# Gate products of feed-forward block i paired with the up products of block i-1, and a new constant for the pace of exponentials in the build-time model

## The chip, the cores and the metric

The kernel runs on one core of a Trainium2 chip, in one launch. The metric is device time in microseconds: 844.57 as the median of four runs (843.4 to 848.04). In the text PE is the matrix engine, DVE the vector engine, ACT the scalar engine, POOL the GpSimd engine, and SP the engine that issues most of the DMAs.

## What is computed

An input x of 2048 rows and 512 columns goes through multi-head attention (32 heads of width 16, no mask) and, beside it, through a feed-forward layer of width 1792 with a SiLU gate. A sigmoid of one dot product for each row mixes the two. All arrays are bfloat16.

```python
qkv = (x @ wqkv).reshape(B, S, 3, H, Dh).transpose(2, 0, 3, 1, 4)      # B=1, S=2048, H=32, Dh=16
p = softmax(einsum("bhqd,bhkd->bhqk", q, k) * Dh ** -0.5)
a = einsum("bhqk,bhkd->bhqd", p, v).transpose(0, 2, 1, 3).reshape(B, S, D) @ wo
b = (silu(x @ w_gate) * (x @ w_up)) @ w_down                            # 512 -> 1792 -> 512
g = sigmoid((x * gate_w).sum(-1, keepdims=True))
return g * a + (1 - g) * b
```

## The kernel before

**Attention.** Queries are cut into four blocks of 512 (`qb`) and heads into eight groups of four (`g`); a pair (qb, g) is a unit, and there are 32 units of 16 key tiles of 128 keys, so 512 tiles of four heads each. A tile goes one of two ways. On the ACT way (`emit_pair`, L698, twice for a tile) PE makes the scores of two heads into a 128x1024 tile `s_t`, of which there are two, and ACT takes the exponential of it into `e_t`. On the DVE way (`emit_d`, L731) PE makes the four scores of a tile one by one into a 128x512 bank `d_t`, and DVE makes the exponential by arithmetic on the bits: four times `y_t<-d_t`, then over 2048 columns `z_t`, a line `u_t`, its square, its product with `z_t`, a POOL DMA that adds it to `y_t`, and a last scaling. The scratch tile of the line bears the name `u_t`, `kaug` or `wd_t`, after where it lies. PE then multiplies either kind with the values into `o_ps` (`pv`, L838).

**Banks.** `d_t`, the feed-forward products and all small products share three PSUM banks (`ps_m`, handed out by `m_tile`, given back by `m_free`).

**Feed-forward.** For each of the four query blocks there are 14 blocks of 128 gate and up columns, 56 in all. `gu_chain` (L619) makes the products of one block with `two_banks` (L378): eight pieces, each a pair of matmuls that run beside each other on the two halves of the array's rows, one into the gate's bank `gu_a` and one into the up's bank `gu_b`. After the last piece ACT takes `th` = tanh(gate/2), DVE makes `gs` = (th + 1) * gate, and then `mt` = 0.5 * gs * up. Both banks are held until DVE has read them. After 14 blocks the products with w_down follow (`down_pieces`, L653, banks `dps_a` and `dps_b`, copied out into `bblk`). The chains run one after the other: each has the one before in its list `after`, and is ready only when that one's pieces are out and all that it owes to DVE has been put in order.

**The order of the work.** The order of the instructions on PE, DVE and ACT is worked out at build time and written as a fixed order (`ordered`, L145). A small model (`Plan`, L276) counts on a clock for each engine: `spend` for PE, `spend_v` for DVE, and on ACT `plan.act`, by `ACT_US` = 0.935 for each exponential of 128x1024 and 0.48 for a tanh. The loop at L1300 puts a pair of scores when the model says that a tile `s_t` comes free, and fills the room before that (`room`, L1310) with DVE-way scores, products with the values, and pieces of the chains. DVE's work waits in the lists `owed` (by a due time), `d_wait`, `vops` and `added`, and `fill_dve` (L802) puts it as long as DVE's clock is behind PE's. `v_unit` (L1267) says whether DVE may take a further tile from the end of a unit: its clock and its work in hand plus `LEAD` = 16 us must lie before the end of that unit's exponentials, counted by `TILE_US` = 1.87 for each tile left.

**Weights.** `load` issues on SP's queue the two 128 KB loads of a block, two blocks ahead, into three buffers each for `wg` and `wu`.

**The end.** `tail` (L939) puts in order what is left of the chains before the last product with the values, and half of the last output products.

Of the kernel before, what the change touches and what calls it, by code (L numbers as in the profile page):

```python
# [9 lines left out]
ALU = mybir.AluOpType  # L10
AX = mybir.AxisListType
BF16 = mybir.dt.bfloat16
# [66 lines left out]
def kernel(  # L79
# [12 lines left out]
    nc = tc.nc  # L92
    P = 128
    x = A_x.flatten_outer_dims()
    S, D = x.shape
    F = B_w_gate.shape[1]
# [4 lines left out]
    DC = D // P  # L101
    FC = F // P
    KT = S // P
    QBW = 512
    QB = S // QBW
# [26 lines left out]
    work = ctx.enter_context(tc.tile_pool(name="work", bufs=2))  # L132
    etp = ctx.enter_context(tc.tile_pool(name="etp", bufs=EB))
    vex = ctx.enter_context(tc.tile_pool(name="vex", bufs=1))
    ffnw = ctx.enter_context(tc.tile_pool(name="ffnw", bufs=3))
# [20 lines left out]
    def mm(*args, **kw):  # L156
        return ordered(nc.tensor.matmul(*args, **kw))  # L157
# [10 lines left out]
    vec = Ordered()  # L168


    xT = big.tile([P, DC, S], BF16, name="xT")
# [37 lines left out]
    mt = big.tile([P, FC, QBW], BF16, name="mt")  # L209
# [39 lines left out]
    for h in range(8):  # L249
        c = 2 * (h % 4) + h // 4  # L250
# [38 lines left out]
    def spend(mode, mms, ready=0.0):  # L289

        plan.seq += 1
        work_at.append((plan.pe, mms))
        plan.pe = max(plan.pe + (0.1 if mode != plan.mode else 0.0), ready) + (0.226 if mode == "F" else 0.216) * mms
        plan.mode = mode

    def later(cost, f, ready=None, key=None):

        c = plan.chain
        if c is not None:
            c.owed += 1  # L300
        ready = plan.pe + 0.25 if ready is None else ready
        owed.insert(sum(o[0] <= ready for o in owed), (ready, cost, f, c, key))
# [8 lines left out]
    def pay(i=0):  # L311
        ready, cost, f, c, key = owed.pop(i)
        spend_v(cost, ready, key)
        keep, plan.chain = plan.chain, None
        f()
        plan.chain = keep
        if c is not None:
            c.owed -= 1
            if c.done():
                c.done_at = plan.slot  # L320
# [14 lines left out]
    def m_tile(name):  # L335
        while m_ready() is None:
            stuck()
        i = min((i for i in range(3) if banks[i] is not None), key=lambda i: banks[i])
        plan.pe = max(plan.pe, banks[i])
        banks[i] = None  # L340
        held[i] = ps_m[i].tile([P, QBW], F32, tag=f"m{i}", name=name)
        return held[i]

    def m_free(ps, t):
        i = [h is ps for h in held].index(True)
        banks[i], held[i] = t + 0.2, None
# [11 lines left out]
    def force(c):  # L358
        for a in c.after:
            force(a)  # L360
        while not c.out():
            while c.cond is not None and not c.cond():
                if owed:
                    pay()
                else:
                    for f in at.pop(min(at)):
                        f()
            emit_piece(c)
        while c.owed:
            pay()  # L370
# [7 lines left out]
    def two_banks(n, name, a, b, end, stop=True):  # L378

        st = {}  # L380

        def pc(k):
            v, i = divmod(k, n)

            def f():
                if k == 0:
                    while m_ready(2) is None:
                        stuck()
                    st["a"], st["b"] = m_tile(name + "_a"), m_tile(name + "_b")
                if k == n:  # L390
                    sync(ordered(nc.tensor.nop()), st["half"])
                    spend("R", 0.1 if st["seq"] < plan.seq else 1.5)
                for ps, (w, r), h in ((st["a"], a(i), v), (st["b"], b(i), 1 - v)):
                    rows = slice(64 * h, 64 * h + 64)
                    st["half"] = mm(ps[:, :], lhsT=w[rows, :], rhs=r[rows, :], start=(k == i == 0),
                                    stop=(stop and k == 2 * n - 1), tile_position=(64 * h, 0), skip_group_check=True)
                spend("R", 1)
                st["seq"] = plan.seq
                if k == 2 * n - 1:
                    end(st["a"], st["b"])  # L400
            return f
        return [(1, pc(k), 2 if k == 0 else 0, "R", st if k == n else None) for k in range(2 * n)]
# [213 lines left out]
        later(0.5, end, plan.act + 0.2)  # L616


    def gu_chain(qb, fc):  # L619
        st = {}  # L620

        def load():
            st["wg"] = ffnw.tile([P, DC, P], BF16, tag="wg", name="wg")
            nc.sync.dma_start(out=st["wg"][:], in_=B_w_gate[:, fc * P:(fc + 1) * P].rearrange("(dc p) f -> p dc f", p=P))
            st["wu"] = ffnw.tile([P, DC, P], BF16, tag="wu", name="wu")
            nc.sync.dma_start(out=st["wu"][:], in_=B_w_up[:, fc * P:(fc + 1) * P].rearrange("(dc p) f -> p dc f", p=P))

        def rows(which):
            return lambda dc: (st["w" + which][:, dc, :], xT[:, dc, qb * QBW:(qb + 1) * QBW])

        def done_gu(gp, up):
            th = work.tile([P, QBW], BF16, tag="th", name="th")
            flush_act(plan.pe + 0.4)
            act(out=th[:], in_=gp[:, :], func=ACT.Tanh, scale=0.5)
            plan.act = max(plan.act, plan.pe + 0.25) + 0.48

            def gate():
                st["gs"] = work.tile([P, QBW], BF16, tag="gs", name="gs")
                vec.scalar_tensor_tensor(out=st["gs"][:], in0=th[:], scalar=1.0, in1=gp[:, :],
                                         op0=ALU.add, op1=ALU.mult)  # L640
                m_free(gp, plan.dve)

            def gated():
                vec.scalar_tensor_tensor(out=mt[:, fc, :], in0=st["gs"][:], scalar=0.5, in1=up[:, :],
                                         op0=ALU.mult, op1=ALU.mult)
                m_free(up, plan.dve)
            later(0.6, gate, plan.act + 0.25, (qb, fc))
            later(0.6, gated, plan.act + 0.25, (qb, fc))
        return load, two_banks(DC, "gu", rows("g"), rows("u"), done_gu)

    scaled = set()

# [65 lines left out]
        pairs[0] += 1  # L718

    exps = []  # L720
    ACT_US = 0.935

    def flush_act(before=None):

# [214 lines left out]
    def tail(k):  # L939

        if k == 0:
            assert here_done and len(scaled) == TQ
            for c in list(pace.chains):
                force(c)
            al = ps_s.tile([P, 2 * QBW], F32, tag="s", name="al")
            a_ps.extend([al[:, 0:QBW], al[:, QBW:2 * QBW]])
        todo = [(tq, i) for tq in (2, 3) for i in range(NB + 1)]
        for tq, i in todo[:5] if k == 0 else todo[5:]:
            w, r = last_rows(tq)(i)
            mm(a_ps[tq][:, 0:D], lhsT=w, rhs=r, start=(i == 0), stop=False)  # L950
# [130 lines left out]
    gates = [pace.add(gate_pieces(2 * i), 36 + 7 * i, 44 + 7 * i) for i in range(KT // 2)]  # L1081
    gates = [pace.add([(0.2, gate_end, False)], 40, 106, gates)]

    gu = {(qb, fc): gu_chain(qb, fc) for qb in range(QB) for fc in range(FC)}
    order_ = [(qb, fc) for qb in range(QB) for fc in range(FC)]
    prev = []
    fin_prev = []
    f0, f1 = 72, SLOTS - 8
    per = (f1 - f0) / QB
    for qb in range(QB):  # L1090
        a0 = f0 + per * qb
        for fc in range(FC):
            load, pcs = gu[(qb, fc)]
            i = order_.index((qb, fc))
            ahead = order_[i + 2] if i + 2 < len(order_) else None

            def first(f=pcs[0][1], load=load, i=i, ahead=ahead):
                if i == 0:
                    load()
                    gu[order_[1]][0]()  # L1100
                if ahead:
                    gu[ahead][0]()
                f()
            pcs = [(pcs[0][0], first) + pcs[0][2:]] + pcs[1:]
            c = pace.add(pcs, 58, a0 + per * (0.6 if qb < QB - 1 else 0.68) * (fc + 1) / FC, prev)
            prev = [c]
        for tq in range(0, TQ, 2):
            c = pace.add(down_pieces(qb, tq), 0 if qb else 100, a0 + per * (0.6 + 0.3 * (tq + 2) / TQ if qb < QB - 1 else 0.68 + 0.32 * (tq + 2) / TQ), prev + fin_prev + gates)
            prev = [c]
        last = qb == QB - 1  # L1110
        fin_prev = []
        if last:

            def ripe():
                return (all((qb, b) in normed for b in range(NB - 1)) and len(scaled) == TQ and here_done)
            pace.add(last_pieces(), SLOTS - KT // 2, SLOTS, prev, cond=ripe)
            break
        for tq in range(0, TQ, 2):
            rel = (UNIT.index((qb, G - 1)) + 1) * KT + 24
            dl = max(a0 + per * (0.9 + 0.1 * (tq + 2) / TQ), rel + 7 + 3 * tq)  # L1120

            def cond(qb=qb):
                return all((qb, b) in normed for b in range(NB))
            fin_prev.append(pace.add(fin_pieces(qb, tq), rel, dl, prev + fin_prev, cond=cond))
# [309 lines left out]
```

## Time and profile before

| what | number |
|---|---|
| median of four runs | 844.57 us |
| time of the profiled execution | 844.66 us |
| its span, first to last instruction | 842.9 us |
| granted PE clock | 0.997 |
| exponentials on ACT (`e_t<-s_t`) | 846, for 423 tiles |
| scores for DVE (`y_t<-d_t`) | 356, for 89 tiles |
| first exponential starts, last starts | 18.5 us, 833.4 us |
| tanh on ACT (`th<-gu_a`) | 56, from 143.8 to 789.6 us |
| gate and up matmuls | 448 and 448, from 132.4 to 788.5 us |
| down matmuls | 448, from 274.8 to 825.1 us |
| loads of `wg` and `wu` | 56 and 56 of 128 KB, on SP's queue |

A row of the profile names the line (a helper records every instruction of an engine, so most have one line), the engine, the operation, the tile written and those read, the count, and then the busy time and the mean time of one. In the timeline a row starts with its start and its length in us, and like instructions that follow each other are one row. A list of waits gives who waited, for whom, the total, the number of times and the longest.

### The profile page before, as it was taken

The page shows a single profiled execution, that of the slowest core. Times are in us where ns is not written, and L with a number is a line of the kernel's source. Part 1 is how long each engine was busy: PE and PEld are TensorE (multiplying, and loading weights), DVE is VectorE, ACT ScalarE, POOL GpSimd, SP SyncE. Part 2 cuts the span into 40 slices and gives each one's busy share as a digit, 9 for nine tenths or more (in the row PEclk, how much of TensorE's full clock was granted, in tenths as well). Part 3 has the DMA queues.
Part 4 walks back from the last instruction along what each step waited for, and adds up shares of the span by engine and source line. Part 5 has one row for each costly group of instructions (what it writes and reads, how often), then busy time and mean ns, then how long its engine had stood idle before and what let it go on. Part 6 is the DMA issues. An engine that isn't in the chain of part 4 may idle for free.

```text
span 842.9 us, 16224 instructions
## 1 busy us (share of the span) xinstructions
PE 764.3 (91%) x6047; PEld 262.4 (31%) x6076; DVE 795.9 (94%) x1159; ACT 815.4 (97%) x912; POOL 93.3 (11%) x122
## 2 busy tenths in 40 slices
PE   7999998999888998989899989899899898988997
PEld 3222233332232332223223323223333233332332
DVE  6999998999999999999999899999998999999996
ACT  3999999999999999999999999999999999999996
POOL 5010100010011010111010100100100110111000
PEclk9999999999999999999999999999999999999999
DMA  9432445345454434554444354454532464354232
GB/s 205 126 66 48 85 80 113 64 93 110 94 102 97 81 68 105 108 109 96 95 93 84 76 113 92 87 115 84 108 80 55 80 133 96 76 118 97 57 69 51
DMA packets 101415, 78.23 MB, mean 93 GB/s; under 512 B 77760, under 2 KB 89624, under 8 KB 101336
## 3 DMA queue, kind: packets, MB, share of 16 engines
q0 software_dynamic: 12672, 46.14, 28.8%
q1 hardware_dynamic: 86792, 30.60, 15.5%
q8 instruction: 47, 0.77, 0.4%
q10 hardware_dynamic: 1872, 0.46, 0.2%
q14 instruction: 32, 0.26, 0.1%
HBM read 20.83 MB, written 2.34 MB: 27 GB/s over the span
## 4 chain that ended last, share of the span: by engine, by line
DVE 28%; PE 14%; ACT 7%; issue 3%; DMA 2%; SPq 0%; DVEq 0%; ACTq 0%
DVE y_t L166 10%; ACT e_t L160 6%; DVE kaug L166 5%; DVE u_t L166 4%; PE s_t L157 4%; PE o_ps L157 2%; DVE z_t L166 2%; DVE gs L166 2%; DVE mt L166 2%; PE dps_b L157 2%; PE d_t L157 1%; PE dps_a L157 1%; PE gu_b L157 1%; DVE osb L166 1%; DMA y_t<-u_t 1%
## 5 line engine op out<-in xcount | busy, mean ns | idle before, releaser
L160 ACT ACTIVATE e_t<-s_t 128x1024 bf16<-128x1024 f32 x846 | 792.2, 1105 | 8.0 <-PE s_t L157 6.4
L157 PE MATMUL s_t<-qx,kaug 64*128 64x512 bf16 x1376 | 293.6, 380 | 34.9 <-ACT e_t L160 29.6
L166 DVE TENSOR_SCALAR y_t<-d_t 128x512 uint16<-128x512 f32 x356 | 234.8, 683 | 16.5 <-PE d_t L157 13.9
L157 PEld LDWEIGHTS <-kaug 64*128 64x128 bf16 x2048 | 136.8, 93 | 323.1 <-issue 287.3
L157 PE MATMUL o_ps<-e_t,vaug 128*32 128x512 bf16 x1692 | 159.9, 390 | 1.6 <-DVE osb L166 1.0
L157 PE MATMUL gu_a<-xT,wg 64*128 64x512 bf16 x448 | 135.5, 376 | 0.0
L157 PE MATMUL gu_b<-xT,wu 64*128 64x512 bf16 x448 | 134.0, 375 | 1.2 <-DVE y_t L166 0.9
L157 PE MATMUL d_t<-qx,kaug 64*128 64x512 bf16 x288 | 107.4, 377 | 16.8 <-DVE y_t L166 8.6
L157 PEld LDWEIGHTS <-vaug 128*32 128x32 bf16 (+1 forms) x2132 | 45.6, 93 | 146.9 <-issue 145.5
L778 POOL DMA_DIRECT2D y_t<-u_t x44 | 40.3, 915 | 350.7 <-PE s_t L157 198.7
L778 POOL DMA_DIRECT2D y_t<-kaug x38 | 35.9, 946 | 310.9 <-PE s_t L157 178.5
L157 PE MATMUL dps_a<-wd_t,mt 64*128 64x512 bf16 x224 | 65.3, 376 | 0.0
L157 PE MATMUL dps_b<-wd_t,mt 64*128 64x512 bf16 x224 | 64.9, 375 | 0.3 <-DVE y_t L166 0.2
L166 DVE TENSOR_SCALAR z_t<-y_t 128x2048 uint16<-128x2048 uint16 x89 | 61.5, 691 | 2.1
L166 DVE TENSOR_SCALAR y_t<-y_t 128x2048 uint16<-128x2048 uint16 x89 | 60.9, 684 | 1.6 <-DMA y_t<-u_t 1.2
L166 DVE TENSOR_TENSOR u_t<-u_t 128x2048 f16<-128x2048 f16 x44 | 53.8, 1223 | 1.1
L166 DVE TENSOR_TENSOR u_t<-u_t,z_t 128x2048 f16<-128x2048 f16 x44 | 53.5, 1217 | 0.1
L157 PE MATMUL s_t<-q,kaug 64*128 64x512 bf16 x212 | 43.4, 386 | 7.5 <-ACT e_t L160 7.0
L166 DVE TENSOR_TENSOR kaug<-kaug 128x2048 f16<-128x2048 f16 x39 | 47.7, 1224 | 0.9
L166 DVE TENSOR_TENSOR kaug<-kaug,z_t 128x2048 f16<-128x2048 f16 x39 | 47.5, 1218 | 0.1
L157 PEld LDWEIGHTS <-wg 64*128 64x128 bf16 x448 | 41.0, 94 | 19.9 <-issue 8.0
L157 PEld LDWEIGHTS <-wu 64*128 64x128 bf16 x448 | 41.8, 94 | 16.1 <-issue 0.5
(131 smaller groups left out, 631.6 us busy)
## 6 DMA issues: line engine op xcount, KB each, us to landing
y_t<-u_t POOLq DMA_DIRECT2D x44, 512.0 KB, 4.8
y_t<-kaug POOLq DMA_DIRECT2D x38, 512.0 KB, 5.0
wg<-in_B_w_gate_dram SPq DMA_DIRECT2D x56, 128.0 KB
wu<-in_B_w_up_dram SPq DMA_DIRECT2D x56, 128.0 KB
y_t<-wd_t POOLq DMA_DIRECT2D x6, 512.0 KB, 4.6
on<-osb SPq DMA_DIRECT2D x120, 16.0 KB
rb<-rr SPq DMA_DIRECT2D x15, 128.0 KB
wd_t<-in_B_w_down_dram SPq DMA_DIRECT2D x7, 256.0 KB
```

The source lines that it names most:

```text
L157: return ordered(nc.tensor.matmul(*args, **kw))
L160: ordered(nc.scalar.activation(*args, **kw))
L166: return lambda *a, **kw: ordered(f(*a, **kw))
L778: nc.gpsimd.dma_start(out=ya, in_=ua, accum_op=ALU.add)
```

## The change

A chain i now holds the gate products of block i and the up products of block i-1. When its pieces are out, `gated` for block i-1 is put among DVE's owed work (its `gs` was made a chain earlier), and the tanh and `gs` of block i follow. There are 57 chains in place of 56: the first has a gate alone, the last an up alone, each as four matmuls over all rows in one bank. The key that kept `gs` and `mt` of one block apart on DVE is gone. At its start a chain issues the load of the up weights of block i+1 and of the gate weights of block i+2; the first also those of `wg` 0, `wu` 0 and `wg` 1. The due times are spread over 15 steps for each query block in place of 14. `ACT_US` becomes 0.906; `TILE_US` stays. In `tail`, the chains are put out in the order of their due times, with all that is owed, ahead of the assertion.

```diff
-    def gu_chain(qb, fc):
...
-        def done_gu(gp, up):
+    FS = [(qb, fc) for qb in range(QB) for fc in range(FC)]
+    w_gate, w_up, gs_of = {}, {}, {}
+
+    def w_load(i, gate):
+        if i < len(FS):
+            w = ffnw.tile([P, DC, P], BF16, tag="wg" if gate else "wu", name="wg" if gate else "wu")
+            fc = FS[i][1]
+            nc.sync.dma_start(out=w[:], in_=(B_w_gate if gate else B_w_up)[:, fc * P:(fc + 1) * P].rearrange(
+                "(dc p) f -> p dc f", p=P))
+            (w_gate if gate else w_up)[i] = w
+
+    def gu_chain(i):
+
+        def rows(w_of, k):
+            return lambda dc: (w_of[k][:, dc, :], xT[:, dc, FS[k][0] * QBW:(FS[k][0] + 1) * QBW])
+
+        def gated(up):
+            vec.scalar_tensor_tensor(out=mt[:, FS[i - 1][1], :], in0=gs_of.pop(i - 1)[:], scalar=0.5, in1=up[:, :],
+                                     op0=ALU.mult, op1=ALU.mult)
+            m_free(up, plan.dve)
+
+        def gate(gp):
             th = work.tile([P, QBW], BF16, tag="th", name="th")
             flush_act(plan.pe + 0.4)
             act(out=th[:], in_=gp[:, :], func=ACT.Tanh, scale=0.5)
             plan.act = max(plan.act, plan.pe + 0.25) + 0.48
 
-            def gate():
...
-            later(0.6, gate, plan.act + 0.25, (qb, fc))
-            later(0.6, gated, plan.act + 0.25, (qb, fc))
-        return load, two_banks(DC, "gu", rows("g"), rows("u"), done_gu)
+            def f():
+                gs = work.tile([P, QBW], BF16, tag="gs", name="gs")
+                vec.scalar_tensor_tensor(out=gs[:], in0=th[:], scalar=1.0, in1=gp[:, :], op0=ALU.add, op1=ALU.mult)
                 m_free(gp, plan.dve)
+                gs_of[i] = gs
+            later(0.6, f, plan.act + 0.25)
+
+        def both(gp, up):
+            later(0.6, lambda: gated(up))
+            gate(gp)
+
+        if 0 < i < len(FS):
+            return two_banks(DC, "gu", rows(w_gate, i), rows(w_up, i - 1), both)
...
-    ACT_US = 0.935
+    ACT_US = 0.906
...
         if k == 0:
+            for c in sorted(pace.chains, key=lambda c: c.deadline):
+                force(c)
+            while owed:
+                pay()
             assert here_done and len(scaled) == TQ
-            for c in list(pace.chains):
-                force(c)
...
+        for i in range(FC * qb + (qb > 0), FC * qb + FC + 1):
+            pcs = gu_chain(i)
+
+            def first(f=pcs[0][1], i=i):
                 if i == 0:
-                    load()
-                    gu[order_[1]][0]()
-                if ahead:
-                    gu[ahead][0]()
+                    w_load(0, True)
+                    w_load(0, False)
+                    w_load(1, True)
+                w_load(i + 1, False)
+                w_load(i + 2, True)
                 f()
...
-            c = pace.add(pcs, 58, a0 + per * (0.6 if qb < QB - 1 else 0.68) * (fc + 1) / FC, prev)
+            c = pace.add(pcs, 58, a0 + per * (0.6 if qb < QB - 1 else 0.68) * (i + 1 - FC * qb) / (FC + 1), prev)
```

More of the change, by code (lines that the diff above doesn't have):

```diff
@@ L616, in gate_end @@
         later(0.5, end, plan.act + 0.2)
-    def gu_chain(qb, fc):
[L620 to L629, printed above, removed]
-        def done_gu(gp, up):
+    FS = [(qb, fc) for qb in range(QB) for fc in range(FC)]
[15 more added lines that the diff above has]
+        def gate(gp):
             th = work.tile([P, QBW], BF16, tag="th", name="th")
@@ L635, in done_gu, with pc, f @@
             plan.act = max(plan.act, plan.pe + 0.25) + 0.48
-            def gate():
-                st["gs"] = work.tile([P, QBW], BF16, tag="gs", name="gs")
-                vec.scalar_tensor_tensor(out=st["gs"][:], in0=th[:], scalar=1.0, in1=gp[:, :],
-                                         op0=ALU.add, op1=ALU.mult)
+            def f():
+                gs = work.tile([P, QBW], BF16, tag="gs", name="gs")
+                vec.scalar_tensor_tensor(out=gs[:], in0=th[:], scalar=1.0, in1=gp[:, :], op0=ALU.add, op1=ALU.mult)
                 m_free(gp, plan.dve)
[L643 to L646, printed above, removed]
-            later(0.6, gate, plan.act + 0.25, (qb, fc))
-            later(0.6, gated, plan.act + 0.25, (qb, fc))
-        return load, two_banks(DC, "gu", rows("g"), rows("u"), done_gu)
+                gs_of[i] = gs
[5 more added lines that the diff above has]
+            return two_banks(DC, "gu", rows(w_gate, i), rows(w_up, i - 1), both)
+        st = {}
+        get, end = (rows(w_gate, 0), gate) if i == 0 else (rows(w_up, i - 1), lambda p: later(0.6, lambda: gated(p)))
+        def pc(h):
+            def f():
+                if h == 0:
+                    st["p"] = m_tile("gu")
+                for dc in (2 * h, 2 * h + 1):
+                    w, r = get(dc)
+                    mm(st["p"][:, :], lhsT=w, rhs=r, start=(dc == 0), stop=(dc == DC - 1))
+                spend("F", 2)
+                if h == 1:
+                    end(st["p"])
+            return f
+        return [(2, pc(0), True), (2, pc(1), False)]
     scaled = set()
@@ L1082 @@
     gates = [pace.add([(0.2, gate_end, False)], 40, 106, gates)]
-    gu = {(qb, fc): gu_chain(qb, fc) for qb in range(QB) for fc in range(FC)}
-    order_ = [(qb, fc) for qb in range(QB) for fc in range(FC)]
     prev = []
@@ L1091 @@
         a0 = f0 + per * qb
[L1092 to L1097, printed above, removed]
-                if i == 0:
-                    load()
-                    gu[order_[1]][0]()
-                if ahead:
-                    gu[ahead][0]()
+        for i in range(FC * qb + (qb > 0), FC * qb + FC + 1):
+            pcs = gu_chain(i)
+            def first(f=pcs[0][1], i=i):
+                if i == 0:
+                    w_load(0, True)
[3 more added lines that the diff above has]
+                w_load(i + 2, True)
                 f()
             pcs = [(pcs[0][0], first) + pcs[0][2:]] + pcs[1:]
-            c = pace.add(pcs, 58, a0 + per * (0.6 if qb < QB - 1 else 0.68) * (fc + 1) / FC, prev)
+            c = pace.add(pcs, 58, a0 + per * (0.6 if qb < QB - 1 else 0.68) * (i + 1 - FC * qb) / (FC + 1), prev)
             prev = [c]
```

## The prediction, made before the run

> **What bounds the kernel now.** I read the page's busy times first, then ACT's timeline in a stretch without disturbance, then the lists of waits of ACT and PE, and last the timelines of one feed-forward block.
>
> ```profile
> span 842.9 us, 16224 instructions
> ...
> PE 764.3 (91%) x6047; PEld 262.4 (31%) x6076; DVE 795.9 (94%) x1159; ACT 815.4 (97%) x912; POOL 93.3 (11%) x122
> ```
>
> Three engines look full. ACT is the fullest, and its work is 846 exponentials and 56 tanh. What one exponential costs must be read with care, since the change turns on it. ACT's timeline (start, length, count):
>
> ```profile
> 486.44 0.72 ACT L160 ACTIVATE th<-gu_a 128x512 bf16<-128x512 f32 x1
> 486.92 8.49 ACT L160 ACTIVATE e_t<-s_t 128x1024 bf16<-128x1024 f32 x9
> 495.19 0.71 ACT L160 ACTIVATE th<-gu_a 128x512 bf16<-128x512 f32 x1
> ...
> 513.68 0.62 ACT L160 ACTIVATE th<-gu_a 128x512 bf16<-128x512 f32 x1
> 514.16 7.48 ACT L160 ACTIVATE e_t<-s_t 128x1024 bf16<-128x1024 f32 x8
> 521.39 0.74 ACT L160 ACTIVATE th<-gu_a 128x512 bf16<-128x512 f32 x1
> ```
>
> By starts, 514.16 to 521.39 is eight exponentials in 7.23 us, 0.904 each: near the new constant. By ends, the tanh ends at 514.30 and the eighth exponential at 521.64, so 7.34/8 = 0.917; likewise 487.16 to 495.41 is 8.25/9 = 0.917, while the starts of that row give 8.27/9 = 0.919. The starts run ahead of the ends for a while and are then held back; the ends keep 0.917. A tanh takes 495.90 - 495.41 = 0.49 by ends. So I count 0.917: 846 x 0.917 + 56 x 0.49 = 775.8 + 27.4 = 803.2 us. The exponentials last from 18.5 to 834.5 (last start 833.4 and 1.17), 816.0 us. **Only 12.8 us of that stretch are ACT stalls.** Before it lie 18.5 us, after it 8.4 (842.9 - 834.5); the execution's 844.66 is 1.8 above its span and 0.1 above the median of the runs.
>
> ACT's list of waits and PE's say who is late:
>
> ```profile
> ACT e_t L160 <- PE s_t L157: 6.4, 14, 1.5
> ...
> PE s_t L157 <- ACT e_t L160: 37.6, 115, 0.8
> PE d_t L157 <- DVE y_t L166: 9.6, 20, 0.9
> PE d_t L157 <- DVE gs L166: 4.0, 11, 1.0
> ```
>
> PE works in a fixed order, so a `d_t` that waits for a bank DVE has not read holds up the next `s_t`, and ACT. I followed back each exponential that ended over 0.04 us late, to the waiting PE row ahead of its scores: about 2.8 us lie before 27 us, in the start; 2.2 behind the copy of a unit's accumulator (`osb`); 5.0 behind banks that DVE had not yet read (`d_t`, `gu_b`, `dps_b`); the rest, near 2.8, in bits. DVE is late because it is loaded to the brim:
>
> ```profile
> 27.00:834.60 807.60, 739.31 (x5868) 252.14 (x5894) 774.86 (x1105) 801.60 (x897) 82.42 (x88) 1.00 0.44 90
> ```
>
> The columns are PE, PEld, DVE, ACT, POOL: DVE is busy 96% of this stretch. The model explains it. With 0.935 it plans 846 x 0.935 + 27 = 818 us for ACT and fills DVE to that length; the chip's 816.0 is that length, though ACT alone could go in 803.
>
> **The change, part by part.**
>
> *0.906.* DVE takes tiles greedily as its clock allows, so their number follows the planned length. What a tile costs DVE can be read start to start:
>
> ```profile
> 309.61 0.69 DVE L166 TENSOR_SCALAR z_t<-y_t 128x2048 uint16<-128x2048 uint16 x1
> 310.34 0.69 DVE L166 TENSOR_SCALAR kaug<-z_t 128x2048 f16<-128x2048 uint16 x1
> 311.07 1.23 DVE L166 TENSOR_TENSOR kaug<-kaug 128x2048 f16<-128x2048 f16 x1
> 312.21 0.68 DVE L166 TENSOR_SCALAR y_t<-d_t 128x512 uint16<-128x512 f32 x1
> 312.81 0.68 DVE L166 TENSOR_SCALAR y_t<-y_t 128x2048 uint16<-128x2048 uint16 x1
> 313.41 1.22 DVE L166 TENSOR_TENSOR kaug<-kaug,z_t 128x2048 f16<-128x2048 f16 x1
> 314.55 0.68 DVE L166 SCALAR_TENSOR_TENSOR gs<-th,gu_a 128x512 bf16<-128x512 bf16 x1
> ...
> 316.01 0.63 DVE L166 SCALAR_TENSOR_TENSOR mt<-gs,gu_b 128x512 bf16<-128x512 bf16 x1
> ```
>
> That is 4 x 0.60 + 0.73 + 0.73 + 1.14 + 1.14 + 0.60 = 6.74. With 89 tiles, DVE's other work and idle time are 818 - 89 x 6.74 = 218. With n tiles and the new pace, ACT's plan is 2 x 0.906 x (512 - n) + 27 and DVE's is 218 + 6.74 n; they meet at n = 736.7/8.55 = 86.2. So three tiles move to ACT: six exponentials, **+5.5 us of true ACT work**, and 20 us off DVE. `TILE_US` stays, and only says how late in a unit DVE may still take a tile. The trace cannot show the planner's choice. Bounds: one tile back to DVE, if the earlier banks feed it (-1.8 us), to five tiles to ACT, if its idle share grows (+9.2). I take two and a half, since the banks help a little: **+4.6 us.** At 0.917 the new constant is too fast by 0.011; the chip's ACT then lags the plan, DVE and PE are ahead of it, and that is cover for their lateness.
>
> The Trainium skill bears on this pace. Its page "Perfetto Trace Analysis" (Optimizing Scalar/DVE Operations) puts ScalarE's engine-busy overhead on PSUM at some 51 ns, and "ScalarE: Activation LUTs" (What ACT_TABLE_LOAD costs) gives 0.833 ns an element: 904 ns for 1024, an estimate that would make 0.906 right. The second page's own form, 186 ns plus the elements less 93 ns of overlap, gives 946 and speaks against it. The ends in the trace, 917, lie between, and decide. By 904 the 851 exponentials of my sum would take 11 us less.
>
> *The pairing.* No work is added on any engine: 448 half-row pairs become 440 and eight full-row matmuls, at about 0.216 each either way; 56 tanh, `gs` and `mt` stay. In the block above the last gate and up matmuls end near 312.0; the up bank is read at 316.01 to 316.6, because its product waits for `th` and then `gs`. After the change `gs` exists already, and DVE's first free place, 312.2 or 312.8, can take it: the up bank comes free some 3 us earlier, 56 times. The gate bank comes free as before, at 315.2; it is what is late next. A chain then owes only up to `gs`, 1 us less than to `mt`, so chains can follow by about 1 us sooner. Nothing new waits on PE. Work on `d_t` that waited for `gs` (4.0 us, 11 times) or `y_t` (9.6) gains. Of the stalls I take away the 5.0 behind banks and 2 of the bits, by DVE's lighter load and the freed bank together: **-7.0 us.** Bounds: 0, and -10 (all but the start).
>
> *Loads.* SP issues the same 112 loads. Up i+1 goes into the buffer of up i-2 and gate i+2 into that of gate i-1, both last read by the chain just ended, as before; so nothing behind them in the queue (the moves of q, k and outputs) waits longer, and each still has two chains (9 us each in the median, by the starts of `th`) to land. Cost 0; if a load blocked, SP would wait for one chain's matmuls, some 3 us, hidden by that lead.
>
> *The end.* The forced order costs nothing while nothing is left: the last `bblk` copies start at 825.5 and 826.2 and the last half-row output product at 830.5, before the last exponential ends. Otherwise each leftover half-row pair costs 0.216 after it. I take 0; bounds 0 and +4.
>
> **Sum:** 842.9 + 4.6 - 7.0 = 840.5 span; with 1.8 around it 842.3, against 844.66. I say 842.3.
>
> **Rivals.**
>
> *The stalls go and no tile moves* (25%). The number of tiles may be set by DVE's four `y` buffers and the banks rather than by its clock. For: DVE's list of waits has 13.9 us for `d_t`, more than for anything else. Against: 96% busy. It gives 844.6 - 8.5 = 836.
>
> *Tiles move and the stalls stay* (23%), slower. Place: ACT between 27 and 834 us. The new constant is the spacing of starts; planned at it, PE's room between two pairs shrinks from 0.935 - 0.216 to 0.906 - 0.216, while its mode changes and matmuls cost what they did; scores come late as often as before, for PE's own sake. Price: three tiles, +5.5, with 12.8 of stalls kept: 850. It decides over the forecast once less than 1.3 us of stalls go for three tiles moved (+4.2, half a per cent). For: some 2.8 us of stalls have no late DVE behind them. Against: PE waits for ACT 37.6 us, so it has room.
>
> *The feed-forward hangs over* (9%). It is one serial chain from 132 to 826 us, ending 8 us before ACT; the plan is 19 us shorter. If pairing doesn't shorten the chain, some 18 slots (4 us) and the last products (2 us) stand after the last exponential: 848.
>
> **How the numbers follow.** The forecast, 838.5 to 846.5, has 43%. The range, 835.5 to 851, takes in the first two rivals' times and leaves out no stalls at all together with no tile moved (834), and five tiles with all stalls (854). Half a per cent, about what a measurement of this kernel can tell from no change, is 4.2 us. Faster: the first rival and 6 of the forecast's 43 make 31%. Slower: the second rival and some of the third make 26%. Same: 43%.
>
> **What would show it.** `e_t<-s_t` x850 to 852 and `y_t<-d_t` x344 to 348; ends of exponentials still 0.917 apart; ACT's excess over 0.917 at 5 to 7 us; `d_t` waiting on `gs` and `y_t` for half as long; DVE busy some 17 us less; `mt<-gs,gu_b` close behind the last matmul; gate and up done before 788. It is wrong if the ends come 0.906 apart, if more than five tiles move, or if down products run past the last exponential.

## The result and the profile after

The changed kernel takes 842.7 us in the median (47 runs, 840.81 to 848.19) against 844.57 (72 runs of the kernel before). The ratio is 0.9976, with a 95% interval of 0.9969 to 0.9983: a real gain of some 2 us, and under half a per cent. The forecast was 842.3. The profile below is of an execution of 843.82 us with a mean granted clock of 0.992, 1.1 above the median.

The page of the profile after, its head and two groups:

```profile
span 842.1 us, 16080 instructions
...
PE 762.9 (91%) x5987; PEld 260.1 (31%) x6020; DVE 785.7 (93%) x1141; ACT 815.5 (97%) x916; POOL 95.2 (11%) x120
...
L160 ACT ACTIVATE e_t<-s_t 128x1024 bf16<-128x1024 f32 x850 | 797.6, 1175 | 7.0 <-PE s_t L157 6.5
...
L166 DVE TENSOR_SCALAR y_t<-d_t 128x512 uint16<-128x512 f32 x348 | 229.0, 682 | 18.7 <-PE d_t L157 15.9
```

850 exponentials in place of 846, and 348 scores for DVE in place of 356: two tiles moved from DVE to ACT, and DVE is busy 10 us less. ACT has 3.7 us more to do (4 x 0.917), and the span is 0.8 shorter nevertheless, so stalls must have gone. PE's list of waits after:

```profile
PE s_t L157 <- ACT e_t L160: 51.2, 158, 1.0
PE o_ps L157 <- DVE osb L166: 2.9, 4, 1.0
PE bp L157 <- DVE mt L166: 1.9, 2, 1.6
PE d_t L157 <- DVE y_t L166: 1.6, 5, 0.6
```

`d_t` waits on `y_t` 1.6 us in place of 9.6, and the 4.0 us on `gs` are gone (0.9 us on `mt` are new); PE waits on ACT 51.2 us in place of 37.6. PE and DVE now run ahead of ACT, and ACT sets the pace. Busy times by stage show where (columns: stage, its length, PE, PEld, DVE, ACT, POOL, granted clock, DMA share, GB/s); first the kernel before, in its start and middle, then the kernel after, in its start and middle:

```profile
100.00:120.00 20.00, 19.17 (x140) 6.01 (x138) 19.90 (x30) 20.00 (x23) 2.13 (x3) 1.00 0.44 83
120.00:140.00 20.00, 18.02 (x149) 6.07 (x150) 17.12 (x27) 19.24 (x22) 2.47 (x3) 1.00 0.51 110
...
220.00:500.00 280.00, 254.09 (x2072) 87.03 (x2077) 269.50 (x379) 277.86 (x312) 29.52 (x32) 1.00 0.45 93
```

```profile
100.00:120.00 20.00, 17.65 (x122) 5.26 (x121) 18.69 (x26) 18.41 (x21) 2.02 (x2) 0.91 0.42 76
120.00:140.00 20.00, 17.71 (x134) 5.58 (x134) 16.36 (x28) 18.06 (x20) 1.72 (x2) 0.91 0.33 65
...
220.00:500.00 280.00, 258.41 (x2111) 91.44 (x2113) 269.98 (x381) 280.00 (x318) 30.35 (x31) 1.00 0.47 96
```

In the middle ACT is busy all of 280.00 us. What stalls are left lie early. Counted as in the prediction, as what the exponentials' stretch is longer than its count at 0.917 and 0.49: 8.3 us of stalls in place of 12.8. Taking only the exponentials that ended over 0.04 us late, those after 200 us fell from 8.9 to 0.9 us and those before rose from 4.3 to 8.0, to which the rows at 100 to 140 us with their clock of 0.91 belong.

One block of the feed-forward after, on DVE:

```profile
505.99 0.68 DVE L166 SCALAR_TENSOR_TENSOR mt<-gs,gu_b 128x512 bf16<-128x512 bf16 x1
506.59 1.22 DVE L166 TENSOR_TENSOR u_t<-u_t 128x2048 f16<-128x2048 f16 x1
507.72 0.42 DVE L166 TENSOR_TENSOR on<-on,rb 128x512 bf16<-128x512 bf16 x1
508.06 0.68 DVE L166 SCALAR_TENSOR_TENSOR gs<-th,gu_a 128x512 bf16<-128x512 bf16 x1
```

Its last gate and up matmuls start at 505.41. The product `mt` that reads the up bank follows at once, and `gs` comes after it, where before the change it came ahead. Over all blocks, from the start of the last up matmul to the end of `mt` it takes 1.45 us in the median, before 4.25; from the start of the last gate matmul to the end of `gs` 2.87, before 3.26. From tanh to tanh a block takes 7.83 us in place of 8.83, as the median of the spacings under 18 us. That median moves by whole exponentials (8 x 0.917 + 0.49 = 7.83; with 9 it is 8.74). The mean of all spacings but the three long ones, in which the down products run, says more: 9.36 us in place of 9.98, 0.6 less for each block. The last tanh of the feed-forward stands at 776 us, before at 790.

### The profile page after: what moved, and what is told of

Same layout as the page of the kernel before. It is cut to its first block, busy times and chain, and to the rows that moved or that the text cites. A ratio compares the mean times of both kernels' runs of the same rounds, so it can differ in the third digit from the quotient of the medians.

```text
span 842.1 us, 16080 instructions
## 1 busy us (share of the span) xinstructions
PE 762.9 (91%) x5987; PEld 260.1 (31%) x6020; DVE 785.7 (93%) x1141; ACT 815.5 (97%) x916; POOL 95.2 (11%) x120
## 5 line engine op out<-in xcount | busy, mean ns | idle before, releaser
L157 PE MATMUL s_t<-qx,kaug 64*128 64x512 bf16 x1376 | 279.9, 381 | 51.0 <-ACT e_t L160 44.5
L166 DVE TENSOR_SCALAR y_t<-d_t 128x512 uint16<-128x512 f32 x348 | 229.0, 682 | 18.7 <-PE d_t L157 15.9
L157 PEld LDWEIGHTS <-kaug 64*128 64x128 bf16 x2048 | 140.0, 93 | 342.6 <-issue 308.3
L157 PE MATMUL gu_a<-xT,wg 64*128 64x512 bf16 x440 | 132.4, 375 | 0.0
L157 PE MATMUL d_t<-qx,kaug 64*128 64x512 bf16 x288 | 105.6, 379 | 4.1 <-DVE y_t L166 1.6
L166 DVE TENSOR_TENSOR kaug<-kaug 128x2048 f16<-128x2048 f16 x37 | 45.2, 1222 | 0.9
L157 PEld LDWEIGHTS <-wg 64*128 64x128 bf16 (+1 forms) x444 | 41.2, 94 | 15.6 <-issue 1.8
L157 PEld LDWEIGHTS <-wu 64*128 64x128 bf16 (+1 forms) x444 | 41.2, 94 | 12.8 <-issue 0.9
L166 DVE TENSOR_TENSOR kaug<-kaug,z_t 128x2048 f16<-128x2048 f16 x37 | 45.0, 1215 | 0.0
```

Source lines behind the costliest of these rows:

```text
L166: return lambda *a, **kw: ordered(f(*a, **kw))
```

## The experiments

The two parts of the change can be set apart, since `ACT_US` is one number. Stalls and tail are read from each run's trace in the same way: "stalls" as above, "tail" from the end of the last exponential to the end of the span. They belong to the one execution that was profiled, which can lie off the median (most for e8: 846.74 against 850.22).

**The pairing alone, the constant alone, and the chip's own pace.** The pairing with the old constant, and with 0.917:

```diff
-    ACT_US = 0.906
+    ACT_US = 0.935        # e1; 0.917 in e3
```

The kernel before with the new constant (e2), or with 0.917 (e4), and the new order of leftovers, which leaves the instructions of the kernel before as they are:

```diff
-    ACT_US = 0.935
+    ACT_US = 0.906        # e2; 0.917 in e4
...
+            for c in sorted(pace.chains, key=lambda c: c.deadline):
+                force(c)
+            while owed:
+                pay()
             assert here_done and len(scaled) == TQ
-            for c in list(pace.chains):
-                force(c)
```

> The pairing alone: the changed kernel with ACT_US = 0.935 kept. Its order holds 844 exponentials on ACT and 90 tiles on DVE. ACT's bare work by ends is 844 x 0.917 + 27.4 = 801.3 us; with 18.5 before, 8.4 after and 1.8 around the span that is 830.0 plus stalls. Theory (the stalls go because the new constant takes work off DVE): DVE is still filled to the planned 818 us, so 9 to 13 us of stalls stay, mostly behind banks that DVE has not read: 839 to 843. Rival (the stalls go because the up bank comes free sooner): 4 to 6 us of stalls, 834 to 836, and d_t waits on gs and y_t fall as in the changed kernel (13.6 us to about 2).

> The constant alone: the kernel before with ACT_US = 0.906, gate and up of the same block, and the new order of leftovers in tail. Its order holds 850 exponentials and 87 tiles on DVE, as the changed kernel. ACT's bare work is 850 x 0.917 + 27.4 = 806.9 us, so 835.6 plus stalls. Theory (the constant removes the stalls): 5 to 8 us of stalls, 841 to 844, the changed kernel's time. Rival (the pairing removes them): 12 us of stalls, 847 to 849, slower than before. A third reading: feed-forward work is left over at the end, so the time after the last exponential grows from 8.4 us to 12 or more.

> The changed kernel with ACT_US = 0.917, the spacing of the ends. 846 exponentials and 89 tiles on DVE, as before the change. Bare: 846 x 0.917 + 27.4 = 803.2, so 831.9 plus stalls. Theory (stalls depend on how far the plan of ACT lies below or above the truth): with the plan at the truth DVE has no cover, 6 to 9 us of stalls, 838 to 841, faster than both kernels by 2 to 5 us. Rival (the pairing removes the stalls): 4 to 5 us, 836 to 837. If more tiles on DVE bring all stalls back: 844.

> The kernel before with ACT_US = 0.917 and the new order of leftovers in tail: 848 exponentials, 88 tiles on DVE. Bare: 848 x 0.917 + 27.4 = 805.0, so 833.7 plus stalls. Theory: 7 to 10 us of stalls, 841 to 844. Rival (only the pairing removes stalls): 12 to 13 us, 846 to 847.

| kernel | exponentials | stalls us | tail us | median us | ratio to before, interval |
|---|---|---|---|---|---|
| before | 846 | 12.8 | 8.4 | 844.57 | |
| changed | 850 | 8.3 | 8.5 | 842.7 | 0.9976, 0.9969 to 0.9983 |
| e1 pairing, 0.935 | 844 | 14.7 | 8.4 | 846.36 | 1.0006, 0.9992 to 1.0020 |
| e2 no pairing, 0.906 | 850 | 9.3 | 29.1 | 865.07 | 1.0234, 1.0219 to 1.0248 |
| e3 pairing, 0.917 | 846 | 12.2 | 8.7 | 844.58 | 0.9985, 0.9972 to 0.9999 |
| e4 no pairing, 0.917 | 848 | 5.8 | 8.9 | 840.65 | 0.9939, 0.9923 to 0.9955 |

Neither part, with the number it has in the change, is worth anything alone. The pairing alone hands DVE one tile more and leaves the stalls: the rival that it removes them fell. Stalls and time even lie above what was expected (14.7 us against 9 to 13; 846.36 against 839 to 843). Its list of PE's waits:

```profile
PE s_t L157 <- ACT e_t L160: 29.0, 92, 0.9
PE d_t L157 <- DVE mt L166: 9.9, 14, 1.1
PE d_t L157 <- DVE y_t L166: 7.5, 25, 0.8
```

`d_t` waits on DVE for 17.4 us here, against 13.6 before; the wait now ends with `mt` where it had ended with `gs`. The constant alone takes the stalls between 200 and 780 us from 7.5 to 3.1, but misses the main expectation by over 20 us, by the third reading: the feed-forward is not done when ACT is. DVE's timeline at its end:

```profile
837.27 0.69 DVE L166 SCALAR_TENSOR_TENSOR mt<-gs,gu_b 128x512 bf16<-128x512 bf16 x1
843.69 0.75 DVE L166 TENSOR_SCALAR bblk<-dps_a,ge 128x512 bf16<-128x512 f32 x1 [5.73 <-PE dps_b L157]
844.36 0.74 DVE L166 TENSOR_SCALAR bblk<-dps_b,ge 128x512 bf16<-128x512 f32 x1
850.97 0.75 DVE L166 TENSOR_SCALAR bblk<-dps_a,ge 128x512 bf16<-128x512 f32 x1 [5.86 <-PE dps_b L157]
```

The last exponential had ended at 834.4. The last block of the feed-forward ends at 838, and both down chains stand bare behind it, near 7 us each. With 0.917 alone, the last such copy starts at 822.4, in time, and the run is faster than the changed kernel, and a little better than expected (5.8 us of stalls, 840.65; 7 to 10 and 841 to 844 expected): the largest gain of these four comes without the pairing. With the pairing, 0.917 missed (838 to 841 expected): 6.0 of its 12.2 us of stalls lie between 30 and 200 us, where the clock fell to 0.85 for 20 us and one `d_t` waited 3.0 us for a DVE write. The number fits the third reading, all stalls back behind DVE, but the place does not: after 200 us exponentials are late by 3.2 us, against 9.9 in e1. Why this order has the wait of 3.0 us, and e4's has not, stays open.

**Where the chain is cut, and where the stalls come from.** e5 is e2 with a chain that does not wait for `mt`; e6 is the kernel before, with 0.935 and the new order of leftovers, and DVE's work planned dearer; e7 and e8 are e4 with 0.926 and 0.912.

```diff
+            keep = plan.chain                  # e5
+            if fc < FC - 1:
+                plan.chain = None
...
             later(0.6, gated, plan.act + 0.25, (qb, fc))
+            plan.chain = keep
...
-        plan.dve = max(plan.dve, ready) + cost          # e6
+        plan.dve = max(plan.dve, ready) + 1.04 * cost
```

> The constant alone (0.906, gate and up of one block), but a chain no longer waits for the product mt of its block before the next may begin (except the last block of each 14, which the down products need): it owes only up to gs, as in the pairing. The up bank is still held until mt is made. 852 exponentials, 86 tiles on DVE. Bare: 852 x 0.917 + 27.4 + 28.7 = 837.4 plus stalls. Theory (what the pairing gives is a shorter serial chain: 8.74 us from tanh to tanh in the constant alone, 7.83 with the pairing): period about 7.8, down products done before the last exponential, 8 to 9 us after it, 5 to 9 us of stalls: 842 to 847. Rival (it is the early free bank that shortens the chain): period stays near 8.7, 25 us or more after the last exponential: 858 to 866.

> The kernel before with ACT_US = 0.935 kept, but each piece of DVE work planned 4% dearer (and the new order of leftovers in tail). 852 exponentials, 86 tiles on DVE. Bare: 837.4 plus stalls. Theory (stalls come from DVE planned to the brim): 4 to 7 us of stalls, 841 to 844, and d_t waits on y_t and gs fall from 13.6 us to under 7. Rival (stalls hang on the constant itself, by the room it gives PE between two pairs): 11 to 13 us of stalls, 848 to 850.

> The kernel before with ACT_US = 0.926 and the new order of leftovers in tail: 848 exponentials, 88 tiles, as with 0.917 alone. Bare 833.7 plus stalls. Theory (stalls grow with the excess of the planned pace over 0.917): between 5.8 (at 0.917) and 12.8 (at 0.935), so 8 to 10: 842 to 844. Rival (the stalls are an accident of each order): any value, and 0.917 alone was luck: 5 or less, or 12 or more.

> The kernel before with ACT_US = 0.912 and the new order of leftovers in tail: 850 exponentials, 87 tiles. Bare 835.6 plus stalls. With 0.917 alone the feed-forward ended in time, with 0.906 alone some 20 us late. Theory (the chain is late by degrees as the plan gets shorter): 6 us of stalls and 0 to 10 us more at the end: 841 to 852. Rival (it is late because work before the feed-forward is forced together, and starts 30 us later): start of the first tanh at 144 or at 176 decides, 841 to 843 or 860 and over.

| kernel | exponentials | stalls us | tail us | last `bblk` starts | median us | ratio to before, interval |
|---|---|---|---|---|---|---|
| e5 | 852 | 5.1 | 23.0 | 843.8 | 858.57 | 1.0159, 1.0146 to 1.0172 |
| e6 | 852 | 3.4 | 12.1 | 831.0 | 845.42 | 1.0007, 0.9997 to 1.0016 |
| e7, 0.926 | 848 | 7.4 | 10.9 | 829.3 | 843.33 | 0.9974, 0.9964 to 0.9984 |
| e8, 0.912 | 850 | 5.0 | 14.5 | 833.1 | 850.22 | 1.0047, 1.0029 to 1.0064 |

My theory of the chain fell in e5: tanh to tanh stayed at 8.81 us (in the mean 9.73, against 9.90 in e2), so what a chain owes is at most a small part of what paces it. e6 settles where the stalls come from: with the constant untouched and DVE planned 4% dearer they go from 12.8 to 3.4. PE's waits there:

```profile
PE s_t L157 <- ACT e_t L160: 56.6, 156, 1.0
PE bp L157 <- DVE mt L166: 1.9, 2, 1.6
PE d_t L157 <- DVE y_t L166: 1.5, 4, 0.5
```

The same picture as in the changed kernel, from the other side of the plan: it is DVE's planned load against ACT's that matters for these waits, and 0.906 was one way to move it. Without the pairing, the lateness after 200 us goes from 8.9 at 0.935 to 5.0 at 0.926, 3.0 at 0.917 and 1.4 at 0.912, with 3.4 at 0.906. The gain is lost at the end (the time of 841 to 844 was missed): the last down copy starts at 831.0 and the last exponential ends at 830.9. In e2, e5, e6 and e8 the span ends 11.9 to 12.0 us after the last down copy starts (863.5 - 851.6; 855.7 - 843.8; 843.0 - 831.0; 845.0 - 833.1), so there the feed-forward ends the kernel, not ACT. For e8 the chain was late by degrees, as the theory had it: first tanh at 151 us, between 143 (0.917) and 176 (0.906). In e7 stalls are 7.4, between e4's 5.8 and 12.8, a little under what was expected.

**The early bank, and a version that beats both.** e9 is the changed kernel with `mt` of block i-1 put behind `gs` of block i, so that the up bank stays held; e10 to e12 are the pairing with 0.935 and DVE's work planned 2, 3 and 4% dearer.

```diff
         def both(gp, up):                      # e9
-            later(0.6, lambda: gated(up))
             gate(gp)
+            later(0.6, lambda: gated(up), plan.act + 0.25)
...
-    ACT_US = 0.906                             # e10, e11, e12
+    ACT_US = 0.935
...
-        plan.dve = max(plan.dve, ready) + cost
+        plan.dve = max(plan.dve, ready) + 1.02 * cost      # 1.03 in e11, 1.04 in e12
```

> The changed kernel, but the product mt of block i-1 is put among the owed work after the gs of block i, with the due time of the tanh; so the up bank is held as long as before the change, though gate and up come from different blocks. 854 exponentials, 85 tiles on DVE. Bare: 854 x 0.917 + 27.4 + 28.7 = 839.2 plus stalls. Theory now (what shortens the chain is the up bank coming free early): tanh to tanh goes back from 7.83 to 8.5 us or more, the last down copy comes after 830, and the time is 850 or more. Rival (the shift of one block itself, or the earlier first block, is what counts): period near 7.8, feed-forward done in time, 843 to 846.

> The pairing with ACT_US = 0.935, and each piece of DVE work planned 2% dearer. 846 exponentials. Bare 831.9 plus stalls. Theory (stalls come from DVE planned to the brim; the pairing keeps the feed-forward in time): 5 to 9 us of stalls, 8.4 us after the last exponential: 837 to 841, and faster than the kernel before.

> As the run before with 3%. 848 exponentials. Bare 833.7 plus stalls. Theory: 4 to 7 us of stalls, 838 to 841.

> As the run before with 4%: the counterpart with pairing of the run that planned DVE 4% dearer without it (3.4 us of stalls, 12.1 us after the last exponential). 850 exponentials. Bare 835.6 plus stalls. Theory: 3 to 5 us of stalls and 8.4 us after the last exponential, 839 to 841. If the pairing does nothing for the end, 12 us after it and 843.

| kernel | exponentials | stalls us | tail us | last `bblk` starts | median us | ratio to before, interval |
|---|---|---|---|---|---|---|
| e9 | 854 | 5.8 | 16.0 | 839.0 | 853.24 | 1.0103, 1.0088 to 1.0118 |
| e10, 2% | 846 | 4.4 | 8.4 | 813.3 | 836.71 | 0.9909, 0.9895 to 0.9922 |
| e11, 3% | 848 | 3.2 | 8.5 | 814.9 | 837.32 | 0.9912, 0.9898 to 0.9926 |
| e12, 4% | 850 | 2.5 | 8.8 | 815.3 | 839.68 | 0.9945, 0.9931 to 0.9959 |

With the bank held (3.44 us from the start of the last up matmul to the end of `mt`), the pairing's gain goes: 8.64 us from tanh to tanh, two tiles fewer for DVE, and a tail of 16.0. The means, without the long spacings, sort all the kernels: 9.22 to 9.46 us with the early bank (the changed kernel, e1, e3, e10 to e12), whatever the constant, 9.82 in e9, and 9.73 to 10.11 in the seven without the pairing. So it is the early free up bank that shortens the chain and lets the feed-forward end in time. In e10 to e12 the last down copy starts 12 to 13 us before the last exponential ends, stalls are near their floor (2.4 us lie before 30 us in each), and the times grow with the count of exponentials. e10 and e11 came out a little better than expected (837 to 841 and 838 to 841). PE's waits on DVE for `d_t` in e10, against 17.4 us in e1:

```profile
PE d_t L157 <- DVE mt L166: 4.2, 10, 0.8
PE d_t L157 <- DVE y_t L166: 1.6, 7, 0.5
```

The best, e10, saves 8.3 us in its own comparison (845.02 to 836.71). Its page:

```profile
span 834.9 us, 16228 instructions
...
PE 766.4 (92%) x6072; PEld 258.4 (31%) x6072; DVE 791.6 (95%) x1159; ACT 812.3 (97%) x912; POOL 98.7 (12%) x122
...
L160 ACT ACTIVATE e_t<-s_t 128x1024 bf16<-128x1024 f32 x846 | 792.5, 1141 | 2.7 <-PE s_t L157 2.0
...
L166 DVE TENSOR_SCALAR y_t<-d_t 128x512 uint16<-128x512 f32 x356 | 231.8, 680 | 13.5 <-PE d_t L157 11.0
```

The engines hold the same 846 exponentials and 356 scores as the kernel before, in another order, and it is 8 us shorter. e3 holds these counts too, and its plan has nearly the same ratio of the two costs (0.935/1.02 = 0.917), yet it stalls for 12.2 us, most of it before 200 us; so the ratio alone does not fix what an order loses early.

## Why the prediction was right, point by point

*The pace by ends.* Right, and it carries all the rest. In a stretch of the changed kernel in which ACT never idles, its timeline reads:

```profile
506.59 0.86 ACT L160 ACTIVATE th<-gu_a 128x512 bf16<-128x512 f32 x1
507.07 12.30 ACT L160 ACTIVATE e_t<-s_t 128x1024 bf16<-128x1024 f32 x13
519.06 0.80 ACT L160 ACTIVATE th<-gu_a 128x512 bf16<-128x512 f32 x1
```

The tanh ends at 507.45 and the thirteenth exponential at 519.37: 11.92/13 = 0.917. The estimate of 904 ns from the Trainium skill ("Perfetto Trace Analysis", Optimizing Scalar/DVE Operations, with the per-element time of "ScalarE: Activation LUTs", What ACT_TABLE_LOAD costs) fits the closest spacing of the starts alone (0.903 over eight); by ends, no eight in a row of either kernel come closer than 0.916.

*Tiles.* +4.6 us forecast, +3.7 measured (850; forecast 850 to 852). The meeting point of the two plans gave 86.2 tiles, the changed kernel holds 87. That the earlier bank gives a part of a tile back holds at 0.935 (the pairing alone has 90 in place of 89), at 0.917 (89 and 88) and with DVE 4% dearer (87 and 86); at 0.906 both orders hold 87. DVE's busy time fell by 10.2 us, where I had said some 17.

*Stalls.* -7.0 forecast, -4.5 measured: the term that was mis-sized. Where DVE held banks the step was right, and even timid: lateness after 200 us went from 8.9 to 0.9, and `d_t` waits on `y_t` and `gs` from 13.6 to 1.6 where I had said half. What it left out is the start: 4.3 to 8.0 us before 200 us. I had bounds of 0 and -10 and no new stall. The order at 0.906 has a wait of PE of 1.04 us for DVE's copy `osb` near 105 us and one of 1.12 us for `aq`, which DVE makes from the next queries, near 132 us. e2, e5 and e9, also at 0.906, have both, and e4, at 0.917, neither. In e9, whose clock stayed at 1.00 there, the exponentials behind them are 0.58 and 1.18 us late, and the kernel before has 0.86 near 130 us. So by my estimate the order itself costs 0.9 us more, and the other 2.8 of the 3.7 go with PE's clock, which fell in the profiled execution after these two waits and after one near 22 us that every kernel here has (last section). The second rival had this in part, scores that come late, but its reason, PE's own sake, was not it: PE waited for DVE, and then ran at a lower clock.

*The sum.* That it came within 0.4 us is in part luck. For the execution whose terms were read it is 844.66 + 3.7 - 4.5 = 843.9 (843.82 measured), 1.5 above the forecast; the median lies below that execution. A slip at the range's lower end changed nothing: no stalls at all with no tile moved would be 844.7 - 12.8 = 831.9; the 834 keeps the stalls of the start.

*Which part does it.* I gave the stalls to "DVE's lighter load and the freed bank together". The runs give them to the load: e1 frees the bank and keeps 14.7 us, e6 lightens the load alone and keeps 3.4. Of the pairing I had a chain shorter by about 1 us for each block. The mean says 0.6 (9.98 to 9.36), and the reason, what the chain owes, was wrong in the main: e5 took that away alone and gained 0.2 us for a block, e9 held the bank and lost the gain. That the bank comes free some 3 us earlier was right (4.25 to 1.45).

*Loads.* 0 was right: the lists of waits of PE and of its weight loads after the change name neither `wg` nor `wu`.

*The end.* 0 was right for the changed kernel. But the third rival, the feed-forward hanging over, is what the constant does without the pairing, and its price was 20.7 us (29.1 - 8.4), not 6: the first tanh came 32 us later (176 in place of 144), which I had not thought of, and whole down chains were left instead of 18 slots.

*The first rival* (stalls go, no tile moves, 836) does not describe the changed kernel, but e10 to within a microsecond: 846 exponentials, 4.4 us of stalls, 836.71.

## What to carry to other kernels

In an order written at build time, an engine's cost constant is a lever on the balance of load, not only a fact. Read an engine's pace from its ends, not from its starts, and give the engine that feeds the bound one a few per cent of air (with the pairing and 0.935, 2% took the stalls from 14.7 to 4.4 us). Setting the constant at the pace of the ends was the best without the pairing (e4) and gained next to nothing with it (e3); no run joined it with dearer DVE work. Before the plan is made shorter, look at which serial chain of side work ends last: here, at 0.906, the up bank held 2 us longer in each block (3.44 in place of 1.45, e9) turned a gain of 2 us into a loss of 8, and without the pairing at all the loss was 20 (e2).

## What the runs showed of the hardware

PE's granted clock fell for a few microseconds after some of its own gaps. PE's timeline of the changed kernel:

```profile
104.82 0.40 PE L157 MATMUL o_ps<-e_t,vaug 128*32 128x512 bf16 x4 [1.04 <-DVE osb L166]
...
106.67 0.61 PE L157 MATMUL d_t<-q,kaug 64*128 64x512 bf16 x2
107.21 0.62 PE L157 MATMUL o_ps<-e_t,vaug 128*32 128x512 bf16 x4
107.76 0.61 PE L157 MATMUL s_t<-on,kaug 64*128 64x512 bf16 x2
...
108.95 0.39 PE L157 MATMUL s_t<-on,kaug 64*128 64x512 bf16 x2
```

After a gap of 1.04 us, rows of `s_t` that elsewhere last 0.39 take 0.61 for about 3 us (granted clock 0.53 from 105 to 107 us and 0.61 from 107 to 109), and ACT's exponentials that start at 105.9, 108.5 and 109.7 end late, by 0.80, 0.77 and 0.33. The same wait does not always do it. e9 has the one for `osb` too (1.03 us, at 103.6), and its clock stayed at 1.00. Every kernel here has the same wait of 1.64 us near 22 us, behind the same DVE write. From 22 to 26 us the clock was 1.00 in the profiled executions of eleven of the fourteen, and 0.65 in the changed kernel, 0.69 in e1 and 0.77 in e3. The spread of the changed kernel's runs goes with it: 22 runs with a mean granted clock of 0.996 or more have a median of 841.95 us, 16 runs between 0.991 and 0.993 one of 843.9; this is a relation over executions, and that the clock alone makes the difference is not shown. What decides between them was not tried.
